# Batch 0's v through the GpSimd queue with a cast, a new order of the last unit's products, and whole-row stores at the end

## The chip, the cores and the metric

The kernel runs on one core of a Trainium2 chip. The metric is the device time of one execution in microseconds (us). A ratio is computed as the mean time of one kernel's fast runs over the mean time of the other's fast runs of the same rounds, so it is not quite the ratio of the medians quoted beside it.

## The reference

Two stages, cut to what matters. There are 8 batches of 8 heads with 576 tokens of 64 elements, then 4 experts over the 4608 tokens.

```python
phi = lambda x: np.where(x > 0, x, np.exp(x) - 1.0) + 1.0
q_p, k_p = phi(q), phi(k)
kv  = einsum('bhsd,bhse->bhde', k_p, v)
num = einsum('bhsd,bhde->bhse', q_p, kv)
den = einsum('bhsd,bhd->bhs', q_p, k_p.sum(2))[..., None] + 1e-6
x   = (num / den).transpose(0, 2, 1, 3).reshape(4608, 512)

p = domain_probs / (domain_probs.sum(-1, keepdims=True) + 1e-9)
for e in range(4):
    out += p[:, e:e+1] * (np.maximum(x @ w1[e], 0) @ w2[e])
```

## The kernel before

The kernel is a fixed schedule: every engine executes its instructions in the order in which the program emits them. Batch 0's attention has to finish before the expert products can start; the other batches' attention hides between expert products. The start is a list of named steps. `qa0` is ScalarE's part of phi on q's first piece, `qd0` the other part, `qT0` its transposes, `v0` the conversion of the first piece of v. A plain number is that many warming products on TensorE, whose results nobody reads.

```python
"MODE": {'k0': 0, 'q2': 0, 'k3': 2, 'q0': 2, ...},   # 2: phi's max(x+1, 1) on GpSimd, then min on VectorE
"START": (11, 'qa0', 'ka0', 'kd0', 'qa1', 'lka', 'qd0', 'lv', 6, 'qT0', 'ka1', 'lkd', 'qd1', 'v1',
          'kd1', 'v0', 'qa2', 11, 'qT1', 3, 'kv0', ..., 'dma0', ...),

def phi_dve(self, name, i):
    ...  # cut: the mode-1 form
    (nc.gpsimd if MODE.get(f"{name}{i}") == 2 else nc.vector).tensor_scalar(hd, src, 1.0, 1.0, AO.add, AO.max)
    nc.vector.tensor_tensor(out=dst, in0=ee, in1=dst, op=AO.min)
...
# all of batch 0 on the sync queue, as float32:
# q0 q1 k0 k1, k's rest, v0 v1, v's rest, q2 q3 k2 k3 v2 v3
ORDER = [(n, 2 * g + i) for g in range(2) for n in "qkv" for i in range(2)]
for (n, i), home in zip(ORDER, homes):
    b0.load(n, i, home=home)
    if i == 1 and n != "q":
        b0.load_left(n)
```

`dma0` issues the first expert's weights from GpSimd; these loads are already cast to fp16 on the way. The end of the kernel is the second layer of the last unit: seven products (numbered 1 to 7), each for two token blocks. They accumulate in PSUM banks `run` (tag b) and `side` (tag e). VectorE adds each result into an SBUF accumulator, which is then stored.

```python
order = L2ORD if n < len(units) - 1 else (2, 1, 5, 6, 3, 7, 4)
# 1, 6, 7, 4 use run; 2, 5, 3 use side
...
if (j, e) == (NTILES - 1, E - 1):
    if p in (3, 7, 4):      # whole rows after 3, column halves after 7 and after 4
        store(j, ns, {3: slice(0, Dm), 7: c2, 4: c1}[p], True)
```

## Time and profile before

| before | us |
|---|---|
| median of the runs | 499.8 |
| span of the profiled execution | 498.2 |
| first continuous expert products start | 20.03 |
| TensorE idle between 30 and 35 us | 1.64 |
| last accumulate ends | 493.45 |

In the profile PE is TensorE's products and PEld its weight loads; DVE is VectorE, ACT ScalarE and POOL GpSimd; SPq and ACTq are the instruction queues from which SyncE and ScalarE issue transfers. The busy line of the page (busy us, share of the span, count of instructions) says that TensorE is the engine to watch:

```profile
PE 483.7 (97%) x4343; PEld 408.5 (82%) x4343; DVE 378.1 (76%) x800; ACT 337.3 (68%) x680; POOL 357.5 (72%) x339
```

The start, from the timeline of the kernel before. The columns are start, duration, engine, source line, operation, output and input with their shapes, count; in brackets stands the idle time before and what ended it:

```profile
3.63 1.91 POOL L326 TENSOR_SCALAR qp<-rawh 128x512 f16<-128x512 f32 x1 [2.26 <-DMA rawh<-in_q_dram]
...
6.13 0.63 ACT L314 ACTIVATE ee<-rawh 128x512 f16<-128x512 f32 x1 [1.93 <-DMA rawh<-in_k_dram]
...
7.13 0.42 DVE L327 TENSOR_TENSOR qp<-ee,qp 128x512 f16<-128x512 f16 x1
...
7.61 0.40 PE L411 MATMUL psum_qT<-identh,qp 128*128 128x128 f16 x4 [0.48 <-DVE qp L327]
...
7.84 2.54 PE L860 MATMUL warm_ps<-qz 128*128 128x512 f16 x11
...
10.56 0.38 PE L411 MATMUL psum_qT<-identh,qp 128*128 128x128 f16 x4 [0.18 <-DVE qp L321]
...
20.03 6.51 PE L522 MATMUL ph<-xT,w 128*128 128x512 f16 x28
```

GpSimd does its part of q0 as soon as q0 lands. ScalarE starts on k0 when it lands, at 6.13 us. VectorE finishes q0 at 7.55, TensorE transposes it, and transposes q1. The continuous expert products begin at 20.03 us.

The view of stretches gives busy time per engine in each stretch, then the granted TensorE clock, the DMA share and GB/s:

```profile
core 0: us, PE busy (x) PEld busy (x) DVE busy (x) ACT busy (x) POOL busy (x), PEclk, DMA share, GB/s
10.00:15.00 5.00, 4.82 (x42) 2.77 (x41) 4.35 (x10) 4.25 (x11) 4.62 (x6) 1.00 1.12 282
15.00:20.00 5.00, 4.29 (x44) 2.76 (x43) 4.73 (x19) 3.80 (x11) 5.00 (x7) 1.00 1.38 177
30.00:35.00 5.00, 3.36 (x22) 1.82 (x21) 3.72 (x8) 2.02 (x5) 2.24 (x4) 1.00 1.17 218
```

VectorE is almost full from 10 to 20 us. Between 30 and 35 us TensorE is busy for only 3.36 us of 5: the chain of waits shows it waiting there for expert 1's weights and for the sums VectorE makes of them.

The end, from the timeline:

```profile
485.19 1.03 PE L666 MATMUL py<-t,h 128*128 128x256 f16 x8 [0.30 <-DVE acc L568]
...
489.56 1.33 PE L666 MATMUL pe<-w,hs 128*128 128x256 f16 x8
...
490.99 3.77 SPq L555 DMA_DIRECT2D out_dram<-acc  x6
491.00 4.35 ACTq L555 DMA_DIRECT2D out_dram<-acc  x6
...
491.89 1.03 PE L666 MATMUL pb<-t,h 128*128 128x256 f16 x8
...
492.53 0.92 DVE L568 SCALAR_TENSOR_TENSOR acc<-pb,p_sb,acc 128x256 f32<-128x256 f32 x2 [0.25 <-PE pb L666]
```

The first line is the last product of the unit before. Product 3, at 489.56 us, takes 1.33 us where its neighbours take 1.04, because its third input sum from GpSimd is late. Product 4, at 491.89, waited 0.31 us, by the order of the schedule for VectorE to read the bank that product 7 had just filled. Six stores per queue are issued from 490.99 us. The last accumulate ends at 493.45 and the span at 498.18, so 4.73 us follow the last accumulate.

### The profile page before, as it was taken

The numbers are of one execution on the slowest core, as the hardware profiler recorded it, in microseconds if no ns is written. First come the engines' busy times: TensorE is split into PE (matmuls) and PEld (weight loads), VectorE is DVE, ScalarE is ACT, GpSimd is POOL, SyncE is SP. The second block draws the span as 40 slices with busy tenths as digits, with TensorE's granted clock in tenths as the row PEclk, the third lists the DMA queues.
The fourth block names the chain that finished last, engine by engine and source line by source line (L and its number), as shares of the span: only waits on it lengthen the run. The fifth ranks groups of instructions, "written<-read, shape, count | busy, mean of one in ns | idle before, by whom it ended". The sixth has DMA issues, their size and how long they took to land.

```text
span 498.2 us, 11603 instructions
## 1 busy us (share of the span) xinstructions
PE 483.7 (97%) x4343; PEld 408.5 (82%) x4343; DVE 378.1 (76%) x800; ACT 337.3 (68%) x680; POOL 357.5 (72%) x339
## 2 busy tenths in 40 slices
PE   8989989899999999999999999999999999999995
PEld 3546756789898989898989898989898888888884
DVE  5647898788876988598869886888687756775685
ACT  5857969974987488847894789568954565446530
POOL 3734304878977697769776977698669877987773
PEclk9999999999999999999999999999999999999999
DMA  8999974642454234632454245523231020002002
GB/s 244 200 215 246 271 150 124 207 113 57 109 167 128 62 95 144 157 75 76 142 167 84 57 153 147 101 52 95 86 79 29 5 94 1 1 1 86 1 1 86
DMA packets 81880, 53.65 MB, mean 108 GB/s; under 512 B 46176, under 2 KB 75360, under 8 KB 81824
## 3 DMA queue, kind: packets, MB, share of 16 engines
q1 hardware_dynamic: 71520, 41.12, 30.5%
q0 software_dynamic: 9824, 11.27, 12.1%
q8 instruction: 34, 0.56, 0.5%
q10 hardware_dynamic: 480, 0.52, 0.3%
q14 instruction: 22, 0.18, 0.1%
HBM read 45.16 MB, written 9.44 MB: 110 GB/s over the span
## 4 chain that ended last, share of the span: by engine, by line
PE 83%; ACT 6%; DVE 4%; DMA 3%; POOL 1%; issue 1%; POOLq 0%; SPq 0%; ACTq 0%; DVEq 0%
PE py L666 37%; PE pb L731 23%; PE pe L731 17%; DMA w<-in_moe_w_dram 3%; PE py L577 2%; PE psum_kv L423 1%; PE psum_nd L463 1%; DMA rawh<-in_k_dram 1%; ACT u L742 1%; ACT vp L330 1%; ACT psum_ee L314 1%; DVE t L622 1%; DVE h L715 1%; DVE acc L568 1%; ACT h L757 1%
## 5 line engine op out<-in xcount | busy, mean ns | idle before, releaser
L568 DVE SCALAR_TENSOR_TENSOR acc<-py,p_sb,acc 128x256 f32<-128x256 f32 (+1 forms) x382 | 182.6, 488 | 46.4 <-PE py L666 40.1
L715 DVE CUSTOM_DVE_ANT_0 h<-pe,u 128x512 f16<-128x512 f32 x140 | 96.3, 688 | 46.9 <-PE pe L731 25.4
L731 PEld LDWEIGHTS <-w 128*128 128x128 f16 x1120 | 108.6, 98 | 18.4 <-DMA w<-in_moe_w_dram 2.0
L633 POOL TENSOR_TENSOR hs<-h 128x512 f16<-128x512 f16 x64 | 74.3, 1160 | 56.1 <-DVE h L715 55.0
L666 PEld LDWEIGHTS <-h 128*128 128x128 f16 x1024 | 99.6, 98 | 12.8 <-issue 1.4
L666 PE MATMUL py<-w,h 128*128 128x256 f16 x744 | 106.4, 273 | 0.5 <-ACT acc L566 0.5
L742 ACT COPY u<-pb 128x512 f32<-128x512 f32 x140 | 82.7, 591 | 27.5 <-PE pb L731 26.3
L635 POOL TENSOR_TENSOR hs<-hs,h 128x512 f16<-128x512 f16 x64 | 73.9, 1155 | 27.7 <-PE py L666 25.1
L731 PEld LDWEIGHTS <-s 128*128 128x128 f16 x840 | 81.5, 98 | 13.4 <-issue 1.1
L731 PE MATMUL pb<-tt,w 128*128 128x256 f16 x560 | 84.1, 273 | 0.5 <-ACT u L742 0.5
L666 PEld LDWEIGHTS <-hs 128*128 128x128 f16 x768 | 74.3, 98 | 9.1 <-POOL hs L639 0.4
L639 POOL TENSOR_TENSOR hs<-h,hs 128x512 f16<-128x512 f16 x64 | 74.4, 1162 | 3.6 <-PE py L666 3.1
L666 PE MATMUL py<-t,hs 128*128 128x256 f16 x496 | 74.4, 273 | 0.0
L637 POOL TENSOR_TENSOR h<-h 128x512 f16<-128x512 f16 x64 | 74.4, 1162 | 0.0
L757 ACT ACTIVATE h<-pe 128x512 f16<-128x512 f32 x70 | 41.9, 598 | 47.1 <-PE pe L731 46.6
L751 ACT COPY pe<-pb 128x512 f32<-128x512 f32 x70 | 40.2, 574 | 41.4 <-PE pb L731 14.8
L775 ACT ACTIVATE h<-pb 128x512 f16<-128x512 f32 x70 | 41.9, 599 | 8.8 <-PE pb L731 8.7
L731 PE MATMUL pb<-tt,s 128*128 128x256 f16 x280 | 42.0, 273 | 0.4 <-DVE s L605 0.4
L731 PE MATMUL pe<-tt,s 128*128 128x256 f16 x280 | 42.0, 273 | 0.0
L731 PE MATMUL pe<-xT,w 128*128 128x256 f16 x248 | 37.2, 273 | 1.0 <-DMA w<-in_moe_w_dram 1.0
L731 PE MATMUL pe<-xT,s 128*128 128x256 f16 x248 | 37.2, 273 | 0.9 <-DVE h L715 0.9
L731 PE MATMUL pb<-xT,w 128*128 128x256 f16 x248 | 37.2, 273 | 0.1
(120 smaller groups left out, 607.6 us busy)
## 6 DMA issues: line engine op xcount, KB each, us to landing
out_dram<-acc SPq DMA_DIRECT2D x32, 256.0 KB, 2.5
w<-in_moe_w_dram POOLq DMA_DIRECT2D x14, 512.0 KB, 12.1
rawb<-in_v_dram SPq DMA_DIRECT2D x26, 256.0 KB, 2.7
rawb<-in_q_dram SPq DMA_DIRECT2D x26, 256.0 KB, 2.8
rawb<-in_k_dram SPq DMA_DIRECT2D x26, 256.0 KB, 3.2
w<-in_moe_w_dram POOLq DMA_DIRECT2D x4, 256.0 KB, 6.6
rawb<-in_k_dram POOLq DMA_DIRECT2D x4, 256.0 KB, 10.1
rl<-in_q_dram SPq DMA_DIRECT2D x16, 64.0 KB, 2.5
```

Of the source, the lines that this page charges most:

```text
L568: nc.vector.scalar_tensor_tensor(out=acc, in0=ps, scalar=pscal, in1=acc, op0=AO.mult, op1=AO.add)
L633: nc.gpsimd.tensor_tensor(out=hs[0], in0=a21, in1=a22, op=AO.add)
L635: nc.gpsimd.tensor_tensor(out=hs[1], in0=hs[0], in1=a11, op=AO.subtract)
L637: nc.gpsimd.tensor_tensor(out=a21, in0=a11, in1=a21, op=AO.subtract)
L639: nc.gpsimd.tensor_tensor(out=hs[3], in0=a12, in1=hs[1], op=AO.subtract)
L666: nc.tensor.matmul(out=ps, lhsT=lhsT(k), rhs=rhs[:, k], start=first and k == 0, stop=k == FH - 1, skip_group_check=True,)
L715: nc.vector._custom_dve(TENSOR_ADD_SAT, out=out, in0=ps, in1=u, s0=BIG, s1=0.0)
L731: nc.tensor.matmul(out=ps[:, kk], lhsT=lk(kc), rhs=rhs[:, kc], start=first and kk == 0 and kc == 0, stop=kc == 1, skip_group_check=True,)
L742: nc.scalar.copy(u, self.b)
L751: nc.scalar.copy(self.e5, self.b)
L757: nc.scalar.activation(self.h[:, :, 0, 0:NH], self.e5, AF.Relu)
L775: nc.scalar.activation(self.h[:, :, 1, 0:NH], self.b, AF.Relu)
```

## The change

Intent at the start: take v off the sync queue. v0 and v1 are issued first of all on GpSimd, v2 and v3 on GpSimd after a gate, which is a one-column copy that waits for k0. All four arrive as fp16. Intent at the end: alternate the two banks over all seven products, and store whole rows.

```diff
-    "START": (11, 'qa0', 'ka0', 'kd0', 'qa1', 'lka', 'qd0', 'lv', 6, 'qT0', ...
+    "START": (11, 'gk0', 'V2', 'V3', 'qa0', 'ka0', 'kd0', 'qa1', 'lka', 'qd0', 'lv', 6, 'qT0', ...
+    "B0": ('pv0', 'pv1', 'sq0', 'sq1', 'sk0', 'sk1', 'slk', 'slv', 'sq2', 'sq3', 'sk2', 'sk3'),
 ...
+        for x in CFG["B0"]:
+            eng = {"s": nc.sync, "a": nc.scalar, "p": nc.gpsimd}[x[0]]
+            ... # b0.load_left or b0.load on that queue
+            "V2": (b0.load, "v", 2, nc.gpsimd, "hs3"),
+            "V3": (b0.load, "v", 3, nc.gpsimd, "hs3"),
+        def gate(n, i):
+            nc.gpsimd.tensor_copy(out=dump, in_=b0.raw[n, i][:, 0, 0, 0:1])
 ...
-            order = L2ORD if n < len(units) - 1 else (2, 1, 5, 6, 3, 7, 4)
+            order = L2ORD
+            if n == len(units) - 1:
+                order, at = (1, 2, 6, 5, 7, 3, 4), at + NSLOT
 ...
-        if (j, e) == (NTILES - 1, E - 1):
-            if p in (3, 7, 4):
-                store(j, ns, {3: slice(0, Dm), 7: c2, 4: c1}[p], True)
-        elif e == E - 1 and p in (3, 4):
-            store(j, ns)
+        if e == E - 1 and p in (3, 4):
+            store(j, ns, j == NTILES - 1)
```

More of the change, by code (lines that the diff above doesn't have):

```diff
@@ L74 @@
     "APS": ('s', 'e', 'b', 'py'),
-    "START": (11, 'qa0', 'ka0', 'kd0', 'qa1', 'lka', 'qd0', 'lv', 6, 'qT0', 'ka1', 'lkd', 'qd1', 'v1', 'kd1', 'v0', 'qa2', 11, 'qT1', 3, 'kv0', 'qd2', 'qa3', 2, 'kv1', 'qd3', 'ka2', 'dma0', 2, 'qT2', 'kd2', 'ka3', 2, 'qT3', 'v2', 'v3', 'nd0', 'kd3', 6, 'nd1', 'kv2', 'xT0', 'kv3', 'nd2', 'xT1', 'nd3', 'ph0', 'ph1', 'dma1', 'xT2', 'xT3', 'ph2'),
+    "START": (11, 'gk0', 'V2', 'V3', 'qa0', 'ka0', 'kd0', 'qa1', 'lka', 'qd0', 'lv', 6, 'qT0', 'ka1', 'lkd', 'qd1', 'v1', 'kd1', 'v0', 'qa2', 11, 'qT1', 3, 'kv0', 'qd2', 'qa3', 2, 'kv1', 'qd3', 'ka2', 'dma0', 2, 'qT2', 'kd2', 'ka3', 2, 'qT3', 'v2', 'v3', 'nd0', 'kd3', 6, 'nd1', 'kv2', 'xT0', 'kv3', 'nd2', 'xT1', 'nd3', 'ph0', 'ph1', 'dma1', 'xT2', 'xT3', 'ph2'),
+    "B0": ('pv0', 'pv1', 'sq0', 'sq1', 'sk0', 'sk1', 'slk', 'slv', 'sq2', 'sq3', 'sk2', 'sk3'),
 }
@@ L544, in new_py, with store @@
         return ppm.tile([P, Dm], FP32, tag="py", bufs=2, name="py")
-    def store(j, ns, ds=slice(0, Dm), last=False):
-        acc = accs[j, ns][:, ds]
+    def store(j, ns, last=False):
+        acc = accs[j, ns]
         if j < B:
@@ L555, in store @@
                 (nc.scalar if last and u else nc.sync).dma_start(
-                    out=out_b[2 * ns + u, SM:S, ds],
+                    out=out_b[2 * ns + u, SM:S],
                     in_=acc[u * HP : (u + 1) * HP],
@@ L644, in layer2_product @@
         if (j, e) == (NTILES - 1, E - 1):
-            if p == 2:
+            if p == 1:
                 pys[i] = [ppm.tile([P, DH], FP32, tag=tag, bufs=2, name=f"p{tag}") for tag in ("b", "e")]
@@ L794, in unit @@
         return layer1(j, e, hT, phs) + layer2(j, e, hT)
-    ORDER = [(n, 2 * g + i) for g in range(2) for n in "qkv" for i in range(2)]
     def order_of(at):
@@ L870 @@
         b0.alloc_left()
-        homes = ["h"] * 4 + [None] * NRAW + ["u2", "u3"]
-        for (n, i), home in zip(ORDER, homes):
-            b0.load(n, i, home=home)
-            if i == 1 and n != "q":
-                b0.load_left(n)
+        homes = dict(sq0="h", sq1="h", sk0="h", sk1="h", ak0="h", ak1="h", pv0="hs1", pv1="hs1", sv2="u2", sv3="u3")
+        for x in CFG["B0"]:
+            eng = {"s": nc.sync, "a": nc.scalar, "p": nc.gpsimd}[x[0]]
+            if x[1] == "l":
+                b0.load_left(x[2], eng=eng)
+            else:
+                b0.load(x[1], int(x[2]), eng, homes.get(x))
         load_probs(nc.sync, True)
@@ L899 @@
             steps[f"ph{i}"] = partial, i
+        dump = pconst.tile([P, 1], FP32, tag="dump", name="dump")
+        def gate(n, i):
+            nc.gpsimd.tensor_copy(out=dump, in_=b0.raw[n, i][:, 0, 0, 0:1])
+        for n in "qkv":
+            for i in range(4):
+                steps[f"g{n}{i}"] = gate, n, i
         turn["aps"] = list(CFG["APS"])
```

## The prediction

> **What bounds the kernel now.** TensorE: 483.7 of 498.2 us busy (page, busy table), and 3.9 us idle between 60 and 450 us (stretches). The change touches the two ends.
>
> Start: continuous TensorE work begins at 20.03 us, when ScalarE has copied the last piece of batch 0's xT (timeline). TensorE is then idle about 1.6 us between 30 and 35 us, waiting for expert 1's first weights (landed 31.2 us, issued about 18.2) and the VectorE sums made of them (chain of waits, stretches).
>
> End: last product 491.89 us, last accumulate until 493.45, and stores issued back to back on both queues from 490.99 (six each, 0.55 to 0.81 us apiece); the last begins at 494.87 on ScalarE's queue.
>
> **Start, costs.** SyncE loses four issues of about 0.5 us; q2, q3, k2, k3 land earlier. GpSimd gains v0, v1 first (0.72 us an issue), then a gate waiting for k0, then v2, v3 (1.44 us), and only then its part of q0, 1.91 us.
> - The Trainium skill, "DMA: Bandwidth & Descriptors", section "Issuing engines are not separate DMA queues", says all queues run on the same 16 engines and interleave. The trace agrees: where both queues had packets (about 13.3 to 14.7 us) the sync queue's packets fell to about half. First packets follow GpSimd's first weight issue by about 2.5 us, so v0 and v1 move from about 3.9 us, in the way of k0 (landed 6.1 us). The cast saves no transfer time: 512-byte cast packets take 60 ns, the uncast 1 KB packets 46 ns. Estimate: k0 lands 0.5 to 1.5 us later.
> - GpSimd finishes q0's part at k0's landing + 3.5 us, so about 10.1 to 11.1 us (before 5.54). VectorE runs in order and needed it at 7.13 us. VectorE is nearly full from 8 to 20 us (4.35 and 4.73 us of two 5 us stretches), so the attention chain moves by 2.5 to 3.7 us.
> - Weight issues start at about 10.0 to 11.5 us (before 10.76) with less sync traffic beside them: expert 1's weights land at 31.2 +/- 0.7. The later start swallows the 1.6 us of TensorE idle.
> Net at the start: +0.5 to +2.2 us, estimate +1.3.
>
> **End, costs.** The order 1,2,6,5,7,3,4 alternates banks throughout and asks for the slow GpSimd sum (0.39 us wait) a product later; the 0.31 us wait before product 4 goes as well. Fourteen accumulates of 0.46 us then bind, so VectorE ends only about 0.3 us earlier. Four larger stores per queue instead of six take away the issue backlog: the last issue starts about 1 us earlier and may take some tenths longer to land. Net: -0.5 to -1.1 us, estimate -0.8.
>
> **Prediction: 500.3 us, 498.3 to 501.9 in 8 of 10 cases.** Faster by over 2%: 0.01; within 2%: 0.98; slower by over 2%: 0.01.
>
> **What would show it.** k0's landing and ScalarE's exp later than 6.13 us; GpSimd's q0 part at about 8 to 10 us rather than 3.63; VectorE's q0 minimum at 10 to 11 us rather than 7.13; xT finished at 22.5 to 24 us rather than 20.9; TensorE idle between 30 and 35 us down to a few tenths; the last two waits among the final products gone; four stores per queue, the last issued by about 494 us.
>
> **What would make it wrong.** If q0 on GpSimd does not wait behind v2 and v3, or VectorE catches up, the start costs nothing and the kernel gains about 1 us. If weights land a microsecond or more earlier, nothing is gained unless the attention chain also is. If k0 is delayed by 2 us or more, the loss is 2 to 3 us.

## The result, and the profile after

The changed kernel takes 505.03 us in the median (504.04 to 505.79, 4 runs), against 499.92 before. The ratio is 1.0102 with a 95% interval of 1.0084 to 1.0121. That is slower by 1%, outside the predicted range of 498.3 to 501.9. The profiled execution is the slowest of the four (span 504.02).

The granted clock on the page (tenths of full speed, one digit for each of 40 slices of the span) has a dent in the second slice:

```profile
PEclk9799999999999999999999999999999999999999
```

The start, from the timeline of the changed kernel:

```profile
8.26 0.63 ACT L315 ACTIVATE ee<-rawh 128x512 f16<-128x512 f32 x1 [3.87 <-DMA rawh<-in_k_dram]
...
8.29 0.44 POOL L903 COPY dump<-rawh 128x1 f32<-128x1 f32 x1 [5.00 <-DMA rawh<-in_k_dram]
8.68 1.44 POOL L275 DMA_DIRECT2D rawv<-in_v_dram  x2
...
10.14 1.95 POOL L327 TENSOR_SCALAR qp<-rawh 128x512 f16<-128x512 f32 x1
...
12.13 0.60 DVE L328 TENSOR_TENSOR qp<-ee,qp 128x512 f16<-128x512 f16 x1 [2.36 <-POOL qp L327]
...
12.78 0.61 PE L412 MATMUL psum_qT<-identh,qp 128*128 128x128 f16 x4 [6.17 <-DVE qp L328]
13.19 4.90 PE L856 MATMUL warm_ps<-qz 128*128 128x512 f16 x11
17.88 0.49 PE L412 MATMUL psum_qT<-identh,qp 128*128 128x128 f16 x4
...
27.45 6.53 PE L523 MATMUL ph<-xT,w 128*128 128x512 f16 x28
```

Read it downward. k0 lands 2.13 us later (8.26 against 6.13). GpSimd then does the gate, two issues and only after them its part of q0, which had been waiting for nothing else since q0 landed before 3.8 us. VectorE, in order, stands still for 2.36 us and starts q0's minimum at 12.13 instead of 7.13. TensorE has been idle for 6.17 us. The same 11 warming products now last 4.90 us instead of 2.54, and q1's transposes wait behind them until 17.88, although VectorE had q1 ready at 15.83. The continuous products start 7.42 us later.

The stretches answer to those of before:

```profile
10.00:15.00 5.00, 2.22 (x9) 1.12 (x10) 2.00 (x6) 3.01 (x6) 4.98 (x7) 0.63 1.11 222
15.00:20.00 5.00, 5.00 (x28) 2.44 (x27) 2.88 (x7) 0.63 (x3) 5.00 (x6) 0.69 1.25 161
30.00:35.00 5.00, 5.00 (x25) 2.28 (x24) 2.23 (x5) 3.39 (x6) 2.16 (x3) 1.00 1.14 222
```

The granted clock is 0.63 and 0.69 where it was 1.00; in one-microsecond stretches it is 0.50 from 12 to 18 us; the trace's clock records have it fall at 11.26 us and rise at 18.08. TensorE's idle time at 30 to 35 us is gone. The view of waits, TensorE alone, puts one line on top (us in total, times, longest):

```profile
PE psum_qT L412 <- DVE qp L328: 6.2, 1, 6.2
```

The end:

```profile
490.97 1.03 PE L667 MATMUL py<-t,h 128*128 128x256 f16 x8 [0.30 <-DVE acc L569]
...
496.21 1.04 PE L667 MATMUL pe<-w,hs 128*128 128x256 f16 x8
...
497.08 1.04 PE L667 MATMUL pb<-t,h 128*128 128x256 f16 x8
...
497.36 2.47 SPq L556 DMA_DIRECT2D out_dram<-acc  x4
497.37 2.77 ACTq L556 DMA_DIRECT2D out_dram<-acc  x4
497.72 0.92 DVE L569 SCALAR_TENSOR_TENSOR acc<-pb,p_sb,acc 128x256 f32<-128x256 f32 x2
```

Both waits among the last products are gone: from the start of the previous unit's last product to the end of the last accumulate it takes 7.67 us (490.97 to 498.64) where it took 8.26. But 5.38 us follow the last accumulate where 4.73 did.

The profiled spans balance. All numbers are differences, after minus before:

| part | us |
|---|---|
| k0 on ScalarE later (6.13 to 8.26) | +2.13 |
| from k0 to VectorE's q0 minimum (1.00 to 3.87) | +2.87 |
| from there to the continuous products (12.90 to 15.32) | +2.42 |
| from there to the previous unit's last product (465.16 to 463.52) | -1.64 |
| last products (8.26 to 7.67) | -0.59 |
| behind the last accumulate (4.73 to 5.38) | +0.65 |
| sum, and the difference of the spans (498.18 to 504.02) | +5.84 |

The theory to test: the start loses through three things in series, (a) v0 and v1 on a second queue delay k0, (b) v2 and v3 stand ahead of q0's part in GpSimd's order, (c) the wait that follows lets TensorE's clock fall, and the warming products, which are in q1's way, then run at half speed. The end gives back through its stores what its order gains. The main rivals: one of (a) and (b) makes nearly all of it; or the clock is only a bystander, because q1 is late anyway; or the cast, not the queue, delays k0.

### The profile page after: what moved, and what is told of

Read it like the earlier page. It is cut to its first block, busy times and chain, and to the rows that moved or that the text cites. A ratio compares the mean times of both kernels' runs of the same rounds, so it can differ in the third digit from the quotient of the medians.

```text
span 504.0 us, 11597 instructions
## 1 busy us (share of the span) xinstructions
PE 484.7 (96%) x4343; PEld 409.9 (81%) x4343; DVE 377.6 (75%) x800; ACT 337.4 (67%) x680; POOL 360.9 (72%) x344
## 4 chain that ended last, share of the span: by engine, by line
PE 84%; ACT 6%; DMA 4%; DVE 3%; SPq 1%; issue 1%; POOL 1%; ACTq 0%
PE py L667 37%; PE pb L729 22%; PE pe L729 16%; PE py L578 2%; DMA rawb<-in_k_dram 2%; PE psum_nd L464 1%; PE warm_ps L856 1%; DMA qT<-qp 1%; PE psum_kv L424 1%; PE ph L523 1%; DMA rawb<-in_q_dram 1%; DVE acc L569 1%; ACT u L740 1%; ACT vp L331 1%; ACT psum_ee L315 1%; DVE t L623 1%
```

## The experiments

Times are medians, with the kernel before of the same rounds. "Products start" is the start of the continuous expert products in the profiled run, and "q0 minimum" is VectorE's.

| run | time | before | ratio (95%) | k0 on ScalarE | q0 minimum | products start |
|---|---|---|---|---|---|---|
| before | 499.83 | | | 6.13 | 7.13 | 20.03 |
| changed | 505.03 | 499.92 | 1.0102 (1.0084 to 1.0121) | 8.26 | 12.13 | 27.45 |
| e1_end_only | 500.50 | 499.89 | 1.0009 (0.9993 to 1.0025) | 5.72 | 6.72 | 19.93 |
| e2_more_warm | 503.95 | 499.89 | 1.0075 (1.0055 to 1.0095) | 7.97 | 11.83 | 26.33 |
| e3_q0_first | 501.33 | 499.89 | 1.0028 (1.0009 to 1.0046) | 7.77 | 8.78 | 22.44 |
| e4_v01_sync | 502.24 | 499.89 | 1.0040 (1.0021 to 1.0058) | 6.25 | 10.32 | 24.28 |
| e5_q0_first_v01_sync | 501.27 | 500.20 | 1.0027 (1.0002 to 1.0052) | 5.88 | 6.88 | 20.96 |
| e6_less_warm | 504.48 | 500.20 | 1.0083 (1.0068 to 1.0098) | 7.58 | 11.45 | 26.00 |
| e7_warm28 | 502.89 | 500.20 | 1.0048 (1.0031 to 1.0065) | 8.30 | 12.17 | 25.50 |
| e8_order_split | 499.76 | 500.20 | 0.9992 (0.9974 to 1.0010) | 5.96 | 6.96 | 19.86 |
| e9_v01_gpsimd_f32 | 506.00 | 500.11 | 1.0108 (1.0090 to 1.0126) | 9.33 | 13.23 | 28.74 |
| e10_order_c1_early | 499.26 | 500.11 | 0.9980 (0.9966 to 0.9993) | 6.12 | 7.13 | 20.03 |

All of them gave correct results.

### e1: the end alone

The kernel before, with only the new order and the whole-row stores from the diff above.

> The kernel before with only the end of the change (product order 1,2,6,5,7,3,4 and whole-row stores). Theory now: the order takes about 0.6 us out of the last products (the two waits of 0.39 and 0.31 us), the whole-row stores start later relative to the last accumulate and give about 0.6 us back; total 499.6 to 500.0, and the stretch from the last accumulate to the end of the span grows from 4.75 to about 5.4 us. Rival, as predicted before the change ran: 0.5 to 1.1 us faster than before, tail not longer. Second rival: the end makes part of the 5 us loss, time above 500.5.

Measured: 500.50 us against 499.89, an interval that includes no change. In the trace the last products take 7.67 us (485.82 to 493.49) and 5.35 us follow the last accumulate, just as in the changed kernel. So by the trace the order is worth 0.59 us, the whole-row stores cost about as much, and the end has no part in the 5 us that shows; the times alone would allow it up to 1.25 us (1.0025). The median lies above the expected 499.6 to 500.0, at the edge of the second rival; its profiled run had 1.1 us of waits for expert 0's second-layer weights, which the change's end can't cause.

### e2 and e7: keep TensorE busy while it waits

Only the warming products ahead of q0's transposes change, so that TensorE is not idle while q0 is late.

```diff
-  ..., 'qd0', 'lv', 6, 'qT0', ...
+  ..., 'qd0', 'lv', 32, 'qT0', ...      # e2
+  ..., 'qd0', 'lv', 28, 'qT0', ...      # e7
```

> The changed kernel with 32 instead of 6 warming products ahead of the first transposes of q, so that TensorE is not idle while it waits for q0. Clock theory: granted clock stays full between 11 and 18 us, the 11 warming products behind those transposes take 2.5 instead of about 4.7 us, VectorE's q0 minimum stays at about 12.1 us, and the time falls by 1.8 to 2.5 us to about 502.5 to 503.2. Rival, that the late data alone makes the loss: no gain, 505 +/- 0.5.

Measured in e2: the clock stayed full, but the time fell by only about 1.1 us and missed the expected 502.5 to 503.2. The timeline says why: 32 were too many, TensorE reached q0's transposes at 13.26, 0.8 us after VectorE had q0 (12.43), and pushed VectorE's q1 to 16.02. So the same test was run again with 28.

> The changed kernel with 28 instead of 6 warming products ahead of the transposes of q0. In the run with 32 the clock stayed full but TensorE reached the transposes 0.8 us after VectorE had q0. With 28: clock full, transposes of q0 within 0.2 us of VectorE's result, those of q1 about 16.0 to 16.3 us (17.88 in the changed kernel), continuous expert products at about 25.6 us, time 502.9 to 503.6. Rival, that the clock costs nothing: transposes of q1 stay at or after 17 us and the time at 504 or more.

Measured in e7, from its timeline:

```profile
12.17 0.60 DVE L328 TENSOR_TENSOR qp<-ee,qp 128x512 f16<-128x512 f16 x1 [2.36 <-POOL qp L327]
...
12.82 0.40 PE L412 MATMUL psum_qT<-identh,qp 128*128 128x128 f16 x4 [0.45 <-DVE qp L328]
13.06 2.54 PE L856 MATMUL warm_ps<-qz 128*128 128x512 f16 x11
16.02 0.38 PE L412 MATMUL psum_qT<-identh,qp 128*128 128x128 f16 x4 [0.42 <-DVE qp L322]
...
25.50 1.77 PE L523 MATMUL ph<-xT,w 128*128 128x512 f16 x6
```

VectorE's q0 minimum stands at 12.17, within 0.04 us of the changed kernel; k0, GpSimd and v are as late as there. What is mended is TensorE's idle time and with it the clock. The 11 products take 2.54 us again, q1's transposes start 1.86 us earlier and now wait for VectorE, and the products start at 25.50 instead of 27.45. The time, 502.89 us, is 2.1 us below that of the changed kernel (505.03, in other rounds). Of the 2.42 us in the table's third row, 1.99 are therefore the clock's (15.32 against 13.33 from q0's minimum to the products); 0.43 us remain. The traces place them: 0.17 us between q0's minimum and its transposes (0.65 against 0.48; the minimum itself takes 0.60 instead of 0.42), and 0.25 us between q0's and q1's transposes (3.20 against 2.95), where TensorE waits 0.42 instead of 0.18 us for VectorE. Why VectorE takes longer there is not shown. The rival that the clock is a bystander falls.

The Trainium skill, "TensorE: Matmul & The Clock Gate", section "Part 1: The HAM clock gate", says that the array falls to half its clock after at least one idle window of about 3.4 us and recovers after about 3.4 us of sustained work. The granted clock was 0.50. The wait of 6.17 us let it fall, and the wait of 2.08 us in e3's profiled run did not. In e4 a wait of 2.99 us, from 7.8 to 10.8 us, was enough. So a wait below the page's figure can do it here. The stretches at half clock agree with the length: 3.41 us in e4 (10.27 to 13.68) and 6.83 us in the changed kernel (11.26 to 18.08), e6 and e9; the full clock was back 2.88 us after work began again in e4 and 5.30 us after it in the changed kernel. So the stretch at half clock, and with it the loss, can differ between runs of one kernel (see e4).

### e3: GpSimd's part of q0 ahead of the gate

```diff
-  (11, 'gk0', 'V2', 'V3', 'qa0', 'ka0', 'kd0', 'qa1', 'lka', 'qd0', 'lv', ...
+  (11, 'qa0', 'ka0', 'kd0', 'qa1', 'lka', 'qd0', 'gk0', 'V2', 'V3', 'lv', ...
```

> The changed kernel with GpSimd's part of q0 ahead of the gate and of v2 and v3. Queue-order theory: k0 still lands at about 8.2 us, VectorE's q0 minimum moves from 12.1 to about 9.3 us, weight issues from 12.4 to about 10.6 us; TensorE's first wait shrinks from 6.2 to about 3 us. Time 500 (clock stays full) to 502.3 (clock still falls). Rival, that the contention of v0 and v1 makes nearly all of the loss: time stays above 504.

Measured: 501.33 us, within the expectation. The profiled run, in the timeline:

```profile
9.25 0.40 PE L412 MATMUL psum_qT<-identh,qp 128*128 128x128 f16 x4 [2.08 <-DVE qp L328]
9.48 2.54 PE L856 MATMUL warm_ps<-qz 128*128 128x512 f16 x11
```

k0 is still late (7.77), but VectorE's q0 minimum follows it by 1.01 us as before, TensorE waits 2.08 us, the clock stays full, and the products start 5.0 us earlier than in the changed kernel. The order on GpSimd thus costs its own 2.9 us, and with it goes the clock's loss. The rival that contention makes nearly all of the loss falls.

### e4: v0 and v1 back on the sync queue

```diff
-  "B0": ('pv0', 'pv1', 'sq0', 'sq1', 'sk0', 'sk1', 'slk', 'slv', 'sq2', ...
+  "B0": ('sq0', 'sq1', 'sk0', 'sk1', 'slk', 'sv0', 'sv1', 'slv', 'sq2', ...
```

> The changed kernel with v0 and v1 loaded as float32 on the sync queue as before, v2 and v3 still behind the gate on GpSimd ahead of q0's part. Contention theory: k0 lands at 6.1 instead of 8.2 us, VectorE's q0 minimum at about 10.0 us, time 502.9 if the clock still falls, about 500.7 if it does not. Rival, that the order on GpSimd makes nearly all of the loss: gain below 0.7 us, k0 still landing at about 8 us or its delay absorbed.

Measured: 502.24 us, where 502.9 was expected if the clock falls; k0 lands in time for 6.25 us, and the clock does fall in the profiled run:

```profile
6.25 0.63 ACT L315 ACTIVATE ee<-rawh 128x512 f16<-128x512 f32 x1 [2.04 <-DMA rawh<-in_k_dram]
...
10.80 0.61 PE L412 MATMUL psum_qT<-identh,qp 128*128 128x128 f16 x4 [2.99 <-DVE qp L328]
11.20 3.77 PE L856 MATMUL warm_ps<-qz 128*128 128x512 f16 x11
```

So v0 and v1 are what delays k0: over all profiles it is ready at 5.72 to 6.25 us where they are on the sync queue and at 7.58 to 8.30 where they are cast on GpSimd's. This kernel's four runs also test the clock without any change of code. One of them has a mean clock of 0.998, too high for even one stretch of 3.41 us at half speed (which alone takes 0.5 x 3.41 / 499.1 = 0.0034 off the mean), and takes 500.88 us, close to the 500.7 expected without the fall; the others have 0.994 and 0.995 and take 502.18 to 502.91.

The packet records agree on the contention: between 4 and 8 us the sync queue moved 1121 KB before and 653 KB in the changed kernel, where GpSimd's queue wrote 234 KB beside it (read as 468 KB of float32). What v reads is taken from what the sync queue would have moved. (Packet times are given here on the axis of the timelines; those of the prediction lie about a quarter of a microsecond later.) This is what the Trainium skill says in "DMA: Bandwidth & Descriptors", section "Issuing engines are not separate DMA queues": all queues end on the same 16 engines.

### e5: both mends

e3's list and e4's loads together; v2 and v3 still go through GpSimd.

> The changed kernel with both mends: GpSimd's part of q0 ahead of the gate, v0 and v1 on the sync queue as float32. If queue order and contention are the whole cause at the start: k0 lands at about 6.1 us, VectorE's q0 minimum at about 7.1 us, the continuous expert products start at 19.5 to 20.5 us (27.45 in the changed kernel, 20.03 before), the clock never falls, time within 0.5 us of before. Rival, a further cost in the change (the gate copy, the cast of fp16 v, v2 and v3 on GpSimd): start later than 21 us and time 1 us or more above before.

Measured: k0 and q0 are back at 5.88 and 6.88 us and the clock does not fall, but the products start at 20.96 and the time is 1.07 us above before. That misses the expectation: something else in the change costs about 1 us, although the interval almost reaches no change and the time includes the changed end. The timelines of e5 and of e1 (whose start is that of the kernel before) show where. First VectorE's first step on q2 in e5:

```profile
12.16 0.43 DVE L327 TENSOR_SCALAR qp<-rawb 128x512 f16<-128x512 f32 x1 [1.00 <-DMA rawb<-in_q_dram]
```

and in e1:

```profile
10.91 0.42 DVE L326 TENSOR_SCALAR qp<-rawb 128x512 f16<-128x512 f32 x1
```

In e5 VectorE waits 1.00 us for q2 to land; in e1 it doesn't wait. (ScalarE starts on q2 at 12.22 in e5 and at 10.72 in e1.) Before, v2 and v3 were last on the sync queue, behind q2, q3, k2 and k3; with the gate on k0 they compete with those. That the competition delays q2 is read from these two traces, which differ also in the gate copy and the order of issues; no run moved v2 and v3 alone. In the changed kernel as it stands this cost is covered by the later chain.

### e6: fewer warming products

```diff
-  ..., 'v0', 'qa2', 11, 'qT1', ...
+  ..., 'v0', 'qa2', 4, 'qT1', ...
```

> The changed kernel with 4 instead of 11 warming products between the transposes of q0 and of q1. Clock theory: at half clock these 11 products hold TensorE 2 us longer than VectorE's q1 result (15.83 us, the transposes at 17.88); with 4 of them the transposes of q1 start at about 15.9 us and the continuous expert products about 1.5 to 2 us earlier, time about 503 to 503.5. Rival, that VectorE's late chain alone decides: no change, 505 +/- 0.5. Risk: fewer products may let the clock stay low longer and give the gain back.

Measured: 504.48 us, a miss. q1's transposes did start at 15.29 and the products follow q0's minimum by 14.55 us (15.32 in the changed kernel), but the clock came back later behind them: its stretch at half speed is as long as in the changed kernel (6.83 us), but lies from 11.84 to 18.67 us, that is until 7.22 us after the start of q0's minimum instead of 5.95. What fewer slow products give, that takes back in part, so this run says little about the size of the clock's share. e7 is the cleaner test.

### e8 and e10: the end, once more

e8 is the kernel before with the new order and its old split stores. e10 also stores the first column half of two row blocks right after product 2, when it is final.

```diff
-            order = L2ORD if n < len(units) - 1 else (2, 1, 5, 6, 3, 7, 4)
+            order = L2ORD
+            if n == len(units) - 1:
+                order, at = (1, 2, 6, 5, 7, 3, 4), at + NSLOT
 ...
-            if p == 2:
+            if p == 1:            # the two banks are taken with the first product
 ...                              # the rest only in e10:
-            if p in (3, 7, 4):
-                store(j, ns, {3: slice(0, Dm), 7: c2, 4: c1}[p], True)
+            if p in (2, 7, 3, 4):
+                store(j, ns, {2: c1, 7: c2, 3: c2, 4: c1}[p], True)
```

> The kernel before with the new order of the last products but its old, split stores. Theory: the stretch from the previous unit's last product to the last accumulate is 7.67 us (8.26 before), and the tail behind the last accumulate is shorter than the 5.3 us of whole-row stores: about 4.8 to 5.0 us; time 0.2 to 0.6 us below before. Rival, that the tail grows because product 3 now comes second to last and not because of the stores' size: tail 5.3 us as with whole rows, time as before.

Measured in e8: the last products take 7.67 us and 4.91 us follow the last accumulate, so the tail grows mostly with the whole rows (0.44 us more in e1, 5.35) and less with the order (0.18 us, from 4.73 before). The median is 0.44 us lower, but the interval includes no change.

> The kernel before with the new product order, and the first column half of the first two row blocks stored right after product 2, when it is final, and all other stores split by column half. Theory that the tail is set by how much is left to move at the end: last products as in the earlier runs (7.67 us from the previous unit's last product to the last accumulate), tail behind the last accumulate 4.4 to 4.8 us (4.73 before, 4.91 with the order and split stores, 5.35 with whole rows); time 0.5 to 0.9 us below before in the medians. Rival, that issue time per queue sets it (eight issues instead of six): tail 4.9 us or longer, no gain over the split stores.

Measured in e10: 499.26 us against 500.11, ratio 0.9980 with an interval of 0.9966 to 0.9993, so it is faster than the kernel before by about 0.2%, and it has the lowest median; e8 and e10 were not compared with each other. The profiled run, the slowest of its six, shows 7.67 us for the last products (486.27 to 493.94) and 4.55 us behind the last accumulate. Eight issues per queue instead of six did not lengthen the tail.

The traces split the tail into three parts: until the last store's issue begins, from there to the last packet of the stores, and the rest.

| last store | issue begins after the last accumulate | issue to last packet | rest |
|---|---|---|---|
| before, 64 KB | 1.42 | 1.60 | 1.70 |
| e8, 64 KB | 1.39 | 1.81 | 1.72 |
| e10, 64 KB | 1.30 | 1.68 | 1.56 |
| e1, 128 KB | 0.89 | 2.98 | 1.47 |
| changed, 128 KB | 0.88 | 2.72 | 1.78 |

So the whole rows do shorten the issues, by about 0.5 us, but the last and larger store takes about 1.1 us longer from issue to its last packet. In all nine traces with whole rows the tail is 5.2 to 5.7 us, in the three without 4.5 to 4.9.

### e9: v0 and v1 on GpSimd without the cast

```diff
-        homes = dict(..., pv0="hs1", pv1="hs1", sv2="u2", sv3="u3")   # fp16 tiles
+        homes = dict(..., sv2="u2", sv3="u3")                         # float32 tiles
```

> The changed kernel with v0 and v1 still issued first on GpSimd but left as float32 (no cast). Theory that the second queue and not the cast delays k0: k0 still lands at 7.5 to 8.3 us, GpSimd, VectorE and clock as in the changed kernel, time 504 to 505.5. Rival, that the cast's small packets make the delay: k0 lands below 7 us, time 503.5 or less.

Measured: k0 lands for 9.33 us, later than with the cast and later than either theory said; the time, 506.00 us, is above both too. In the packet records v0 and v1 then travel as 128 packets of 4096 bytes at 159 ns (median) instead of 512 packets of 512 bytes at 59 ns. So the second queue delays k0 without any cast; in this single profile the cast even made the delay smaller, and why is not shown. The rival falls.

## Why the prediction was wrong

- **GpSimd's order: right in mechanism.** The step "VectorE runs in order and needed it at 7.13 us", with q0's part at k0's landing plus 3.5 us, was seen: 3.87 us in the changed kernel. The gate took 0.44 us, where 0.15 was left for it (3.5 less 1.44 and 1.91). e3 confirms it by taking it away.
- **k0's landing: mis-sized.** "k0 lands 0.5 to 1.5 us later" became 2.13 us; e4 removes it. The mechanism, shared DMA engines, was right. "The cast saves no transfer time" holds for the packets' own time (512 at 59 ns are more than 128 at 159), but it was no guide to k0: without the cast k0 came 1.07 us later still (e9). The prediction's own clause for a delay "by 2 us or more" gave a loss of 2 to 3 us; the delay came, and the loss was 5.
- **The step that failed: "the attention chain moves by 2.5 to 3.7 us".** It moved by 7.42 us. The sum held only k0's delay and GpSimd's order, which measured 5.00 us together, already 1.3 us above the upper end. And it left out that TensorE has nothing to do meanwhile: idle for 6.17 us, it lost half its clock, and 11 products meant as harmless filler then stood in q1's way. e7 gives that term: 1.99 us. The prediction never asked what the engine that waits would do afterwards.
- **The 1.6 us of idle time swallowed: right.** The part from the continuous products to the previous unit's last product got shorter by 1.64 us, and TensorE is busy for all of 30 to 35 us. The times were off: weight issues began at 12.37 us (10.0 to 11.5 predicted), and VectorE got expert 1's weights at 32.77 (31.2 +/- 0.7), still before TensorE wanted them.
- **The end: "estimate -0.8" was wrong in its sign for the stores.** The order gave 0.59 us (0.3 were predicted). "Four larger stores per queue instead of six take away the issue backlog" did happen: counted from the previous unit's last product, the last issue starts 1.12 us earlier, as predicted. The failed term is "may take some tenths longer to land": from that issue to the last packet it took 2.72 us instead of 1.60. More bytes start later: the first store begins 1.28 us before the last accumulate ends (497.36 to 498.64) where it began 2.46 us before (490.99 to 493.45). So the tail grew by 0.65 us (e1, e8). In sum +0.06 instead of -0.8.
- **v2 and v3** seem to cost about 1 us more once the rest is mended (e5), which the prediction did not have; the cause is read from traces and not shown by a run.

Left open: why VectorE takes the 0.43 us longer between q0's minimum and the products that neither the clock nor the order explains, why k0 comes later without the cast, and what in v2's and v3's move costs e5 its 1 us.

## What to carry to other kernels

A queue that looks free is not free if its engine has work of its own behind the issues, and if its transfers share the DMA engines with the one load that everybody waits for: ask first which load is awaited, then what a second queue puts beside it. When a change makes TensorE wait a few microseconds more, add the price of the clock that falls in that wait, paid by every product that runs next, fillers included. At the end of a kernel, try storing each piece when it is final; here fewer and larger stores that start later lengthened the tail.

## What the Trainium skill lacked or had wrong

- "TensorE: Matmul & The Clock Gate", section "Part 1: The HAM clock gate", gives about 3.4 us of idle time; in e4 the clock fell to 0.50 within a wait of 2.99 us, 2.46 us after the last product had ended (7.81 to 10.27), and in e3 it did not within one of 2.08 us. The page says that its window runs freely; how little work in a window lets the clock fall it does not say.
- No page warns that fillers in front of dependent work, meant to keep the array warm, cost double after a wait: 11 of them took 4.90 us instead of 2.54 us here, and held q1's transposes back by 2.05 us (15.83 to 17.88).
- "DMA: Bandwidth & Descriptors", section "Latency and other measured facts", gives about 1 us to the first byte of a transfer issued on GpSimd. Here the first packet of v0 came 2.28 us after its issue began (1.34 to 3.62 us) and the first weight packet of the kernel before 2.27 us after its own (10.76 to 13.03). The page does not say from where it counts; from the end of these issues (0.89 and 0.98 us long) it is 1.3 to 1.4 us.
- No page compares a cast with an uncast load from GpSimd beside a busy sync queue; here k0 was ready at 8.26 us with the cast (7.58 to 8.30 in five profiles) and at 9.33 us without (one profile).
